# Rebuilt transform tables, a last unit gated by token groups and a new rule in the instruction planner of a fused adaLN, long-convolution and gMLP block

## The chip, the cores and the metric

One core of a Trainium2 chip runs the whole program. A core has five engines with queues of their own: TensorE (PE in the profile, with its weight loads as PEld), VectorE (DVE), ScalarE (ACT), GpSimd (POOL) and SyncE (SP, which here issues nearly all DMAs). Each engine takes its instructions strictly in order and waits on semaphores. The metric is the device time of one execution in microseconds; the median of several runs is compared.

## The reference

The input is x = A_q of 2048 tokens by 640 channels, in bfloat16. Six vectors of 640 come from one small product, `silu(c) @ w_mod`: shift, scale and gate for each of two halves.

```
h = layernorm(x) * (1 + ca) + sa
k_shift = 4-tap causal convolution of k along the tokens, per channel
kv = k_shift * v
y  = irfft(rfft(kv padded to 4096) * rfft(ssm_k padded to 4096))[:2048] + kv * ssm_D
x  = x + ga * h * y
h  = layernorm(x) * (1 + cb) + sb
z  = gelu(h @ w_in);  z1, z2 = halves of z (864 columns each);  z2 = layernorm(z2)
g  = w_sp @ z2 + b_sp            # over the tokens, 2048 x 2048
out = x + gb * ((z1 * g) @ w_out)
```

## The kernel before

**Stages.** The first part, some 224 us, computes everything up to z; the second part (lines 880 to 940) is a plain loop over 16 token tiles of the product with `w_sp` (`mix`, L905) and the product with `w_out` (`project`, L923). The second part isn't touched by the change.

**The long convolution** is done as matrix products. The 640 channels are 5 units of 128 (`NU`, `DU`). For each unit the filter (X named K) and the kv product (X named U) go through the same steps: `load_X` brings 512 KB in; `stage1` multiplies by a small table F1 (four pieces, each evacuated from PSUM to `X1`, L315); `forward` multiplies by slices of a 128 x 128 x 16 table of cosines and sines, `M2`. The filter's result is kept as `KH` (`k_item`). For the kv product, `u_item` multiplies its spectrum by KH on VectorE (`product`, L497, 40 of them), goes back with the transposed table `G2` (`inv`) and evacuates to `Z`. There are 8 such steps per unit. `last_stage` turns Z by a DMA transpose, and `y_mult` multiplies it by the table E and then, on VectorE, `gh` (the modulated first layernorm) by the result (L686). Only the last unit, u = 4, is turned on TensorE (`last_stage_pe`): four blocks of eight transposes, each with a copy to `ZTp` and its own `y_mult`. Each `y_mult` covers 32 channels of all 2048 tokens, so no token is complete before the fourth. Two of these four go through a ScalarE copy first (L681, L683).

**The tables.** `M2` is built in eight chunks (`m2_chunk`): three GpSimd instructions per chunk make the angle in turns and its rounding (L395, L397, L398), two on VectorE take the remainder and its absolute value (L402, L327), two Sin activations on ScalarE follow (L405, L407), and VectorE negates one of the parts (L409). `G2` is made from M2 by TensorE transposes (L422), a VectorE copy (L424) and a negation on GpSimd (L427). A block of G2 needs four chunks of M2, and `forward` step st needs chunk st. Silu, which the modulation vectors need, and a warming Gelu run on ScalarE ahead of these.

**The rest.** `load_kv` and `short_conv` make kv in a transposed layout (`taps` on TensorE with a diagonal `dg`, then `times_v` on VectorE, L561), write it to HBM, and read it as XU. `ln1` (statistics on VectorE, or on ScalarE at L580, L581), `xn`, `mod`, `gh_mod` (L658) and `resid` (L723) are the first layernorm, its modulation and the residual add. `resid` also takes the statistics of the second layernorm (L729), and for each of four token groups of 512 `z_group` finishes these (L795, and `rstd_from_var` on GpSimd, L234 and L235), normalises (L803), turns the tile (group 0 by TensorE with ScalarE modulating, L824 and L831; the others by a DMA transpose with VectorE, L816) and multiplies by `w_in`.

**The planner.** Nothing in the first part is in program order. Each piece of work is an `op` with one or more engines and a cost for each, its dependencies, the buffers it opens, and a wished time `t` from the table `WANT`. `Plan.run` walks forward in its own model of time: among all ops that are ready it picks the one that can start first, adding a handicap from `SECOND` where an op would go to an engine that isn't its first; `t` breaks ties. The order in which ops are picked is the order on the engines. Buffers of a kind come in a number of slots (`SLOTS`); those in `FIXED` are opened in the order in which the code names them. Where the model shows TensorE without work for long, `new` puts in filler products of `ident` with 512 columns (`plan.gap`), which compute nothing that is used and keep TensorE busy.

The key by which the planner chooses, and the line in which it does so:

```
key = (at + (o["alt"] if e != next(iter(o["eng"])) else 0), o["t"], i)
if best is None or key < best[0]:
```

## Time and profile before

| | us |
|---|---|
| median of 5 runs | 353.93 (353.86 to 354.36) |
| the profiled execution | 353.93 |
| its span, first to last instruction | 352.1 |
| TensorE busy, share of the span | 329.5, 94% |
| VectorE busy | 218.0, 62% |
| ScalarE busy | 147.4, 42% |
| GpSimd busy | 111.7, 32% |

The span runs from the first to the last instruction; the device time is 1.8 us longer. A busy TensorE is not a TensorE doing useful work: the fillers count as busy, and a matmul's recorded duration is longer than the time until the next can start. In the tables of instructions an L number is the line in the kernel that issued it; L293 is the helper through which most matmuls go, and L315 the helper for copies, so these are told apart by the names of the tiles (`sm<-ident` is a filler, `ZTp<-pu` the copy of a turned block). GpSimd's spans are rough.

### The profile page before, as it was taken

How to read it: one execution, taken by the hardware profiler on the slowest of the kernel's cores; microseconds unless marked ns; L12 is line 12 of the kernel's file. 1: busy time of each engine (PE TensorE's matmuls, PEld its weight loads, DVE VectorE, ACT ScalarE, POOL GpSimd, SP SyncE). 2: the span in 40 equal slices, each digit the busy share in tenths (PEclk: the TensorE clock that was granted, in tenths of full speed). 3: DMA queues.
4: the chain of work that ended last, by engine and by line, in shares of the span. 5: the costliest groups of instructions: out<-in, count | busy, mean ns of one | idle time of the engine just before them, and what ended most of it. 6: DMA issues, size and time to landing. Idle time of an engine off the chain costs nothing.

```text
span 352.1 us, 6835 instructions
## 1 busy us (share of the span) xinstructions
PE 329.5 (94%) x2819; PEld 211.3 (60%) x2826; DVE 218.0 (62%) x435; ACT 147.4 (42%) x243; POOL 111.7 (32%) x142
## 2 busy tenths in 40 slices
PE   7667999999996999897999999999999999999996
PEld 3235577877885899753555555555555555555554
DVE  7986598867589668999798678623223332232233
ACT  6467897886565675626555555200000000000000
POOL 7775130026899973661211014800000000000000
PEclk9999999999999899998999999999999999999999
DMA  7899993087829198530430896046764655531111
GB/s 123 183 280 253 204 348 83 2 212 197 198 80 231 59 236 166 154 93 2 75 63 13 129 181 190 0 97 144 96 152 104 106 125 121 119 98 47 45 47 56
DMA packets 128342, 45.02 MB, mean 128 GB/s; under 512 B 117592, under 2 KB 127672, under 8 KB 128312
## 3 DMA queue, kind: packets, MB, share of 16 engines
q1 hardware_dynamic: 127008, 44.59, 56.8%
q8 instruction: 22, 0.36, 0.4%
q10 hardware_dynamic: 1304, 0.00, 0.2%
q14 instruction: 8, 0.07, 0.0%
HBM read 16.11 MB, written 5.24 MB: 61 GB/s over the span
## 4 chain that ended last, share of the span: by engine, by line
PE 80%; DVE 8%; ACT 5%; POOL 3%; issue 2%; POOLq 0%; DVEq 0%; ACTq 0%
PE ps L905 27%; PE pz L293 18%; PE pu L293 18%; PE po L923 9%; PE sm L293 5%; PE s L293 4%; ACT X L315 2%; POOL T L398 1%; DVE st L729 1%; DVE T L497 1%; DVE xt L723 1%; DVE gh L686 1%; ACT KH L315 1%; POOL T L397 1%; ACT Z L831 1%
## 5 line engine op out<-in xcount | busy, mean ns | idle before, releaser
L905 PE MATMUL ps<-X,wT 128*128 128x432 bf16 x512 | 95.7, 346 | 0.0
L905 PEld LDWEIGHTS <-wT 128*128 128x128 bf16 x512 | 50.0, 98 | 42.3
L497 DVE TENSOR_TENSOR T<-pu,KH 128x1024 bf16<-128x1024 f32 x40 | 48.5, 1222 | 15.1 <-PE pu L293 10.4
L916 ACT COPY uT<-pt 128x896 bf16<-128x896 bf16 x1 | 0.9, 905 | 118.9 <-PE pt L915 118.9
L293 PEld LDWEIGHTS <-Z 128*128 128x128 bf16 x320 | 31.4, 98 | 27.6 <-issue 0.8
L293 PE MATMUL pu<-X,M 128*128 128x128 bf16 (+1 forms) x480 | 45.7, 239 | 0.2
L293 PE MATMUL pz<-T,G 128*128 128x128 bf16 (+1 forms) x480 | 42.6, 240 | 3.4 <-DVE T L497 3.3
L315 ACT CAST X<-s 128x1024 bf16<-128x1024 f32 x40 | 40.8, 1020 | 11.3 <-PE s L293 10.8
L293 PEld LDWEIGHTS <-G 128*128 128x128 bf16 x480 | 35.7, 99 | 7.3 <-issue 3.6
L293 PEld LDWEIGHTS <-M 128*128 128x128 bf16 x480 | 35.5, 98 | 5.8 <-issue 0.2
L908 DVE SCALAR_TENSOR_TENSOR u<-ps,bcol,G 128x432 bf16<-128x432 f32 x18 | 12.0, 668 | 42.2 <-PE ps L905 42.2
L293 PE MATMUL pu<-big,Z 128*128 128x432 bf16 x160 | 34.6, 348 | 0.0
L293 PE MATMUL pz<-big,Z 128*128 128x432 bf16 x160 | 34.4, 346 | 0.0
L923 PE MATMUL po<-w_o,uT 128*128 128x320 bf16 (+1 forms) x224 | 32.8, 299 | 0.0
L315 ACT CAST Z<-pz 128x512 bf16<-128x512 f32 x40 | 23.5, 590 | 17.2 <-PE pz L293 17.1
L908 DVE SCALAR_TENSOR_TENSOR u<-ps,bcol,M 128x432 bf16<-128x432 f32 x14 | 9.4, 668 | 31.5 <-PE ps L905 31.5
L923 PEld LDWEIGHTS <-uT 128*128 128x128 bf16 (+1 forms) x224 | 21.8, 98 | 9.8
L658 POOL TENSOR_TENSOR gh<-gh,gca_bf 128x512 bf16<-128x512 bf16 x20 | 23.2, 1170 | 9.0 <-DVE gca_bf L645 9.0
L862 DVE BATCH_NORM_STATS2 stz<-X 128x6 f32<-128x432 bf16 x32 | 18.8, 599 | 10.1 <-ACT X L856 9.5
L315 ACT CAST KH<-pu 128x512 bf16<-128x512 f32 x40 | 23.1, 605 | 3.9 <-PE pu L293 3.6
L925 DVE TENSOR_TENSOR ot<-po,xt 128x320 bf16<-128x320 f32 x32 | 15.7, 491 | 13.4 <-PE po L923 13.4
L658 POOL TENSOR_TENSOR gh<-gh,gsa_bf 128x512 bf16<-128x512 bf16 x20 | 23.0, 1160 | 2.7 <-DVE gsa_bf L648 1.6
(132 smaller groups left out, 380.4 us busy)
## 6 DMA issues: line engine op xcount, KB each, us to landing
wm<-in_w_mod_dram SPq DMA_DIRECT2D x6, 800.0 KB, 5.1
X<-in_A_ssm_k_dram SPq DMA_DIRECT2D x5, 512.0 KB, 6.0
kv_scr<-big SPq DMA_DIRECT2D x5, 512.0 KB, 5.5
xt<-in_A_q_dram SPq DMA_DIRECT2D x4, 640.0 KB, 5.7
X<-kv_scr SPq DMA_DIRECT2D x5, 512.0 KB, 4.7
out_dram<-ot SPq DMA_DIRECT2D x16, 160.0 KB, 2.5
big<-in_B_w_in_dram SPq DMA_DIRECT2D x2, 1080.0 KB, 6.3
w_o<-in_B_w_out_dram SPq DMA_DIRECT2D x6, 160.0 KB, 2.9
```

The source lines that it names most:

```text
L293: nc.tensor.matmul(o, lhsT=w, rhs=x, start=start, stop=stop)
L315: (e.copy if e is nc.scalar else e.tensor_copy)(dst, src)
L397: e.tensor_scalar(tl[v][:], tl[v][:], pidx[:, 0:1], 1.0 / 8192.0, op0=ALU.mult, op1=ALU.mult)
L398: e.tensor_scalar(tl[r][:], tl[v][:], MAGIC, MAGIC, op0=ALU.add, op1=ALU.subtract)
L497: e.tensor_tensor(T_[:], tl[pu][:, :, :, None, :].to_broadcast([P, KP, 2, 2, DU]), tl[KH][:, :, None, :, :].to_broadcast([P, KP, 2, 2, DU] ...
L658: lambda e, vec=vec, o=o: e.tensor_tensor(gvu, gvu, vec[:, None, d0:d0 + du].to_broadcast([P, TB, du]), op=o),
L686: op({"DVE": dve_cost(512)}, lambda e: e.tensor_tensor(ghv, ghv, src(), op=ALU.mult), r=[py], w=gk, t=t)
L862: op({"DVE": 620}, lambda e, i=i, n=n, fc=fc: e.bn_stats(out=stz[:, n, fc, :], in_=tl[z2][:, i, fc * FC:(fc + 1) * FC]), r=[(z2, (i, fc))] ...
L905: nc.tensor.matmul(ps[:, :FC], lhsT=wTs[t][:, s_, :], rhs=tl["z2_%d" % (s_ // TB)][:, s_ % TB, fc * FC:(fc + 1) * FC], start=(s_ == 0), st ...
L908: nc.vector.scalar_tensor_tensor(u[:, sl], ps[:, :FC], bcol[:, t:t + 1], z1[t][:, sl], op0=ALU.add, op1=ALU.mult)
L923: nc.tensor.matmul(ps[:, :HS], lhsT=uTs[t][:fsz[ft], ft, :], rhs=w_o[:fsz[ft], ft, h * HS:(h + 1) * HS], start=(ft == 0), stop=(ft == NFT ...
L925: nc.vector.tensor_tensor(ot[:, h * HS:(h + 1) * HS], ps[:, :HS], xt[:, t, h * HS:(h + 1) * HS], op=ALU.add)
```

## The change

**The planner.** `op` gets a mark `port` for VectorE instructions that use the SBUF port that VectorE shares with GpSimd. In the plan, a GpSimd op and a marked VectorE op no longer overlap: each starts at the earliest when the other's is over. The choice among ready ops is no longer strictly by the earliest start: all candidates within `LOOK` = 31 ns of the earliest are compared by their wished time. The wished times are new (`WANT`), several hundred single ops get a correction of their own (`SHIFT`), the handicaps are new (`SECOND`), and many costs are adjusted.

**The tables.** Of M2 the angle is now a common base (`m2_base`, one iota and one multiplication) plus a step per chunk. A chunk is two `tensor_scalar` on VectorE (or GpSimd), one `scalar_tensor_tensor` over 512 elements, two Sin activations that take the step as their bias, and the negation. The negation for G2 and the diagonal of the short convolution may go to VectorE or GpSimd, with VectorE first. Silu and the warming Gelu move behind the last Sin.

**The last unit.** All four blocks are turned and copied first, into the four `T` buffers. Then for each token group of 512 there are 32 matmuls of 16 columns (128 in all instead of 32 of 64 columns) and one VectorE multiplication, which completes that group for the unit.

**Small ones.** In `ln1` the repair of statistics taken on ScalarE is a VectorE op for a whole run of tiles, and `nmr1` is one VectorE instruction instead of two on GpSimd. `norm` of the second layernorm may go to ScalarE. `ZTp` now has one slot, which holds the base.

The diff, without the numbers of the three tables and without adjusted costs:

```diff
+LOOK = 31
-SLOTS = dict(X=4, ..., ZTp=2, ...)
+SLOTS = dict(X=4, ..., ZTp=1, ...)
-SECOND = {"gh": 13421, "h2": 7734, "ln": 256, "res": 1494, "x1": 12998, "xn": 2029, "z": 19661, "zt": 22790}
+SECOND = {"dg": 1178, "g2": 29243, "gh": 23515, "h2": 25688, "ln": 8821, "m1": 16354, "m2": 5123, "res": 1875, "x1": 27814, "xn": 542, "z": 24289, "zt": 20107, "zx": 18935}
...
-                    key = (at + (o["alt"] if e != next(iter(o["eng"])) else 0), o["t"], i)
-                    if best is None or key < best[0]:
-                        best = (key, i, e, cost, max(at, landed) if o["flip"] else at)
+                    if e == "POOL" or (e == "DVE" and o["port"]):
+                        at = max(at, port)
+                    seen = at + (o["alt"] if k else 0)
+                    found.append((o["t"], seen, i, k, e, cost, max(at, landed) if o["flip"] else at))
+            first = min((f[1] for f in found), default=0)
+            best = min((f for f in found if f[1] <= first + LOOK), default=None)
...
+            if e == "POOL" or (e == "DVE" and o["port"]):
+                port = at + cost
...
+        mstep, mturn = small("mstep", 2 * NCH), small("mturn", 2 * NCH)
+        nc.vector.tensor_scalar(mstep[:, 0:NCH], fidx[:, 0:NCH], pidx[:, 0:1], 4.0 * KCH / 8192.0, op0=ALU.mult, op1=ALU.mult)
+        nc.vector.tensor_scalar(mstep[:, NCH:], mstep[:, 0:NCH], 0.25, None, op0=ALU.add)
+        nc.vector.tensor_scalar(mturn[:], mstep[:], TWO_PI, None, op0=ALU.mult)
...
+                new(a, "T", [P, 2, KCH, P], F32)
+                for h in range(2):
+                    e.tensor_scalar(tl[a][:, h], tl["mbase"][:], mstep[:, h * NCH + i:h * NCH + i + 1], MAGIC, op0=ALU.add, op1=ALU.add)
+            op({"DVE": 540, "POOL": 1000}, turns, r=["mbase"], w=[a], new=[(a, "T")], t=t, alt="m2", port=True)
+            op({"DVE": 650}, lambda e: e.scalar_tensor_tensor(tl[a][:], tl[a][:], MAGIC, tl["mbase"][:, None].to_broadcast([P, 2, KCH, P]),
+                                                              op0=ALU.subtract, op1=ALU.subtract), r=["mbase"], w=[a], t=t, port=True)
+            for h, o in ((0, 2), (1, 0)):
+                op({"ACT": 430}, lambda e, h=h, o=o: e.activation(M2[:, o, ks], tl[a][:, h], ACT.Sin, scale=-TWO_PI,
+                                                                  bias=mturn[:, h * NCH + i:h * NCH + i + 1]),
...
-            op({"POOL": 1200}, lambda e: e.tensor_scalar(flatG[:, o:o + 8, :], flatG[:, 8 * b:8 * b + 8, :], -1.0, 1.0,
+            op({"DVE": 350, "POOL": 1050}, lambda e: e.tensor_scalar(flatG[:, o:o + 8, :], flatG[:, 8 * b:8 * b + 8, :], -1.0, 1.0,
...
-            op({"DVE": 650} if dt == 0 else {"POOL": 1100}, diag, ...)
+            op({"DVE": 650} if dt == 0 else {"DVE": 650, "POOL": 1050}, diag, ..., alt="dg", port=True)
...
-                op({"ACT": act_cost(1024), "DVE": 750}, keep, ...)
-                y_mult(u, qb, ZT, 0, ("y%d" % u, b), b % 2 == 0)
+                op({"ACT": act_cost(1024), "DVE": 750}, keep, ...)
+            for g in range(NT // TB):
...
+                    for q in range(NQ):
+                        mm(pv[:, :, q // (NQ // 2), q % (NQ // 2), :], tl[ZTs[q // QB]][:, q % QB, :], Ebd[:, g * TB:(g + 1) * TB, :],
+                           True, True)
+                op(pe(*[16] * NQ), mul, r=ZTs + ["E"], w=[py], ...)
+                op({"DVE": dve_cost(512)}, lambda e, ghv=ghv, py=py: e.tensor_tensor(ghv, ghv, tl[py][:], op=ALU.mult),
+                   r=[py], w=[("gh", (u, g))], ...)
...
-        op({"ACT": 1500}, lambda e: e.activation(sc[:], c_bf[:], ACT.Silu), w=["silu"], t=("", -60))
+        op({"ACT": 1500}, lambda e: e.activation(sc[:], c_bf[:], ACT.Silu), r=["M2", "e2c", "F1"], w=["silu"], t=("silu", 0))
...
+            op({"DVE": 150}, lambda e: e.scalar_tensor_tensor(nmr2[:, gs], mv2[:, gs, 0], -1.0, rstd2[:, gs], op0=ALU.mult, op1=ALU.mult),
+               w=[("nm2", g)], r=[("rs2", g)], t=("zp_%d" % g, 0.5))
```

## The prediction

> **What bounds the kernel now.** First the page's totals and its rows of busy tenths (40 slices of 8.8 us).
>
> ```profile
> PE 329.5 (94%) x2819; PEld 211.3 (60%) x2826; DVE 218.0 (62%) x435; ACT 147.4 (42%) x243; POOL 111.7 (32%) x142
> ...
> PE   7667999999996999897999999999999999999996
> ...
> PEclk9999999999999899998999999999999999999999
> ```
>
> TensorE is the bound, but not evenly: slices 1 to 4, 13 and 17 to 18 are thin. I cut the span there, with the busy time of each engine in each stretch (after start:end come its length, PE, PEld, DVE, ACT, POOL, the granted clock, the DMA share and GB/s).
>
> ```profile
> 0.00:42.00 42.00, 32.26 (x253) 16.71 (x256) 30.74 (x85) 27.96 (x46) 26.12 (x49) 1.00 0.99 211
> 42.00:106.80 64.80, 63.73 (x823) 50.67 (x827) 51.46 (x83) 50.16 (x83) 28.97 (x40) 1.00 0.64 161
> 106.80:118.00 11.20, 8.01 (x103) 6.47 (x99) 9.56 (x9) 5.67 (x8) 10.81 (x11) 0.85 0.84 205
> 118.00:144.50 26.50, 26.42 (x414) 23.90 (x409) 21.29 (x24) 17.31 (x28) 17.96 (x16) 1.00 0.72 157
> 144.50:163.90 19.40, 14.76 (x176) 9.74 (x177) 18.79 (x55) 9.44 (x15) 8.43 (x9) 0.95 0.26 82
> 163.90:223.70 59.80, 59.80 (x325) 31.75 (x324) 47.70 (x116) 35.46 (x65) 15.39 (x19) 0.99 0.49 96
> ```
>
> From 163.9 on TensorE is full, and the change has nothing to take there: 59.8 us for z, then 128.4 to the end. Ahead of it I count what TensorE loses: idle time, fillers, low clock. In 0 to 42 it idles 9.74; of 35 fillers, 19 run slow at the start (5.86 us by the timeline) and 16 take 0.22 each (22 of them took 4.91 later on): 9.74 + 5.86 + 3.6 = 19.2. In 42 to 106.8: 1.1 idle and 8 fillers, 2.9. In 106.8 to 118: 3.2 idle, one filler, and 15% of 8.0 us for the clock, 4.6. In 118 to 144.5: 0.1. In the tail: 4.6 idle, 25 fillers 5.6, clock 0.7, together 10.9. Lost in all 37.7 of 163.9 us; so 126 us of useful work are left, and only the start, the hole and the tail can shrink.
>
> What holds each? For the start, the chain of work that ended last:
>
> ```profile
> 14.34 1.25 POOL dg L546
> ...
> 16.00 0.48 POOL T L397
> ...
> 16.56 1.11 POOL T L398
> 17.67 0.31 POOL T L395
> ```
>
> It runs on GpSimd from 10.5 to 24.0, through L395, L397 and L398 of chunk after chunk. For the hole, the timeline:
>
> ```profile
> 107.06 5.13 DVE L723 TENSOR_TENSOR xt<-xt,gh 128x512 bf16<-128x512 bf16 x4
> ...
> 113.37 1.22 PE L293 MATMUL pz<-T,G 128*128 128x256 bf16 x12 [2.87 <-DVE T L497]
> ```
>
> Four residual adds on VectorE take 5.13 us while GpSimd works; the same form takes 0.36 to 0.44 where GpSimd rests. The product (L497) queued behind them comes late, and TensorE waits 2.87 us. For the tail, the chain again:
>
> ```profile
> 144.51 0.59 ACT Z L315
> ...
> 148.90 1.79 DVE gh L686 x3
> ...
> 154.44 1.29 DVE xt L723
> ...
> 159.11 1.53 DVE Z L803 x4
> ...
> 161.00 2.22 ACT Z L831 x3
> ```
>
> The last inverse product ends at 144.5 and z starts at 163.9; VectorE is busy 18.8 of these 19.4 us, much of it with tokens that group 0 doesn't need.
>
> **What the Trainium skill says.** "SBUF — State Buffer", section Who interferes with whom: a VectorE instruction in a two-port mode, or with two SBUF inputs against a GpSimd one that reads SBUF, blocks fully until the other is over. The trace agrees: 1.25 to 1.37 us for the adds under GpSimd, about one GpSimd instruction (1.16) later. Products from PSUM stay at 1.21 to 1.23 throughout. "TensorE: Matmul & The Clock Gate", What's actually happening, has half clock after some 3.4 us of idleness; the records show 0.85 behind the hole. "ScalarE: Activation LUTs", What ACT_TABLE_LOAD costs, gives 1283 ns for a load; this trace has five of 1.28.
>
> **The change part by part.** Against the profiled execution, 353.93 with its span of 352.1 (1.8 outside it); the median is the same number.
>
> *Tables.* GpSimd loses per chunk 0.355 + 0.496 + 1.101 = 1.95 us, 15.6 in all. VectorE had 0.427 + 0.578 + 0.321 = 1.33 (10.6 in all, with port waits). Now it has two fp32 `tensor_scalar` of 256, a form that no row shows on VectorE: by "VectorE: DVE Perf Modes", section Side-by-side, two elements a cycle and some 150 cycles fixed, 0.29 each (an estimate; 0.42 if it runs at one a cycle, as L327 does). The `scalar_tensor_tensor` over 512: L327's undisturbed 0.42 plus 256 elements at 0.96 GHz, 0.69. The negation undisturbed 0.22. Sum 1.49, 11.9 in all, bounded by 10.5 and 14. `m2` has VectorE first and a handicap of 5.1 us on GpSimd, so I put all of it on VectorE. There too go four G2 negations (1.04 on GpSimd; 0.42 from the 256-element form plus 768 at four per cycle) = 1.7, up to four diagonals at 0.77 = 3.1, and three small step instructions ahead of the plan, 0.6. The E table sheds port waits: its two one-element instructions of 0.87 and 0.51 against 0.16 for their like (L347), 1.1.
>
> VectorE's need from 4.9 us (F1 done) to the end of M2: a diagonal 0.8, E 2.7, M2 11.9, four `times_v` 2.7: 18.1, so 23.0 instead of 26.9, when the last negation ended. Half of it suffices for the first steps. ScalarE is free earlier: its first Sin waited at 8.8 behind three loads for Silu, Gelu and Sin again (3 x 1.28 and two activations of 0.2, from 4.5). The two that stay come behind the last Sin: 3.0 us on ScalarE just where it is busy (8.96 of 10 us in 30 to 40). `times_v` of the first kv tile, which began at 11.63 though its taps ran from 7.9, may begin 3 us earlier, and with it the write, the read of XU and the kv `stage1` (29.6 to 36.8 before). The new wishes also load the first filter block ahead of the second kv tile (-1045 against -53), past SP's four transposes. The first product L497 came at 41.5; VectorE (23), ScalarE (its work up to there is 22 + 3 us from 2.8) and the XU read allow 31 to 36. Not all is gain: some taps that filled TensorE before 20 us come later. I take **-5.5**, bounded by 0 (VectorE simply replaces GpSimd) and -9 (at 31 us about 20 of useful work fit, so 10 are lost instead of 19.2).
>
> *Hole.* With the port rule a GpSimd-first op never starts earlier on VectorE while GpSimd is working, and the handicap of 1.9 us decides for GpSimd. So the five residual adds of units 0 to 3 on VectorE move: +5 x 1.16 = 5.8 us for GpSimd, which has shed 15.6 + 4.1 + 4.4 and so has room; if it had none, residuals would come late, but only the tail waits for them. I take **-3.5** of the 4.6, bounds -4.6 and 0.
>
> *Tail.* From the last inverse product: Z copy 0.6, first flips 0.65, four copies on ScalarE (handicap 20 us on VectorE) 4 x 1.02, 32 matmuls of 16 columns. That size is in no row; eight of 64 columns take 0.23 to the next group, so 0.03 each gives 0.9; the TensorE page (Wait — 56ns, not 53.3ns?) has a floor of 25 ns whatever the size, 0.8, so both ends agree, and the 96 additional matmuls cost 2.8 us, under fillers. Then 0.68 (L686), 0.44 (add), four statistics and aggregates at 0.42 = 1.7, GpSimd 1.5, the new `nm2` 0.2, norm 1.5, flips 0.4, ScalarE modulating 3.7: 16.4 with 0.5 for hops, against 19.4: -3. But z of group 1 must follow: group 0 takes 16 x 0.913 = 14.6 us, to 178.5, and group 1's tile was ready at about 177.4 (its transpose issued at 169.54, 5.8 to landing, five times 0.41). That is 1.1 of slack, and VectorE is busy 24.4 of 25.5 us from 144.5 to 170; nine statistics of later groups (0.37 each) can stand back. I take **-2.5**, bounds -4 and 0.
>
> *Friction.* First-layernorm statistics leave ScalarE (handicap 8.8 instead of 0.26): four tiles at 1.15 = 4.6 us more for VectorE, with two diagonals in 40 to 66, where it was busy 22.6 of 26: 28.7 needed, 2.7 too many; from 33.3 to 42 it was idle 5.4. I take **+1.5**, bounds 0 and +8.
>
> Sum: -5.5 - 3.5 - 2.5 + 1.5 = -10.0. Span 342.1, time **343.9**. Removed table loads, shorter GpSimd rstd and the unused ScalarE norm I cost at nothing: they are covered by TensorE's 102 nearly full microseconds from 42 to 144.5, or are in the sums.
>
> **Rivals.**
> *VectorE replaces GpSimd in the start* (-1 instead of -5.5): for it, VectorE is busy 24.9 of 28.4 us from 4.9 to 33.3 already; against it, half of M2 suffices. 348.4.
> *The tail gives nothing*, since group 1 comes no earlier (slack 1.1): 346.4.
> *Everything works* at its far bound without friction, -9 - 4.6 - 4: 336.3.
> *Slower: VectorE becomes the bound from 5 to 66 us.* It was busy 49 of 61 there. M2 +1.3, G2 +1.7, diagonals +3.1, statistics +4.6, less E's 1.1: 58.6. Being in order, each product behind a batch of these is late, and TensorE waits. The start gains nothing, friction +8, hole -3.5, tail -2.5: +2, 355.9. It decides when friction passes 6 us with no gain in the start. Against it, products stand early in the wishes (t 0 to 40; statistics 3424).
>
> **How the numbers follow.** Forecast 0.43 (its own range 341 to 347), VectorE in the start 0.22, no tail 0.10, everything 0.13, slower 0.10, within 0.2% (353.2 to 354.6, about what this kernel's measurement can tell from no change) 0.02. Faster is 0.43 + 0.22 + 0.10 + 0.13 = 0.88. The range leaves out the slower case and half of the best one: 336.5 to 351.5.
>
> **What would show it.** M2 chunks without GpSimd and its last Sin before 23; first L497 by 36; no VectorE block of adds at over 1 us each; z starting near 154; three table loads. Wrong: TensorE waiting for L497 in 40 to 66, `tensor_scalar` of the chunks above 0.42, fillers as many as before, or TensorE idle between z groups 0 and 1.

## The result and the profile after

| | before | after |
|---|---|---|
| median, us | 354.97 (80 runs) | 354.21 (43 runs) |
| ratio of the two | | 0.9946 [0.9930, 0.9962] |
| profiled execution, us | 353.93 | 354.21 |
| its span, us | 352.1 | 352.2 |

By the ratio the change makes the kernel about 1.9 us faster, where 10 were predicted; the forecast of 343.9 and the upper end of its range, 351.5, both lie below what was measured. Executions of one kernel lie up to 5.7 us apart here (350.12 to 355.78 for the changed one), and the ratio is one of fast runs, which leaves out the ten slowest of the changed kernel and none of the kernel before; over all executions the means are 1.3 us apart and the medians 0.8. So the two profiled executions, which are equally long (that of the kernel before is 1.0 us under its median), are no contradiction to the ratio. They serve to say where time went, and the ratio says how much.

The page of the changed kernel, its totals, TensorE's row of busy tenths and the granted clock:

```profile
PE 332.6 (94%) x2923; PEld 213.7 (61%) x2929; DVE 219.9 (62%) x465; ACT 139.2 (40%) x225; POOL 89.9 (26%) x101
...
PE   7559899999999999997999999999999999999996
...
PEclk9978999999999999998999999999999999999999
```

The dent of the hole (a 6 in the thirteenth place before) is gone, that of the tail (an 8 and a 7) is down to one 7, and GpSimd has lost 21.8 us of work. The thin slices at the left edge are still there, 7559 where 7667 stood. The same stages as in the prediction, with the columns as there:

```profile
0.00:42.00 42.00, 31.54 (x224) 16.18 (x226) 33.46 (x108) 23.42 (x39) 2.56 (x15) 0.92 0.90 192
42.00:106.80 64.80, 63.67 (x784) 48.35 (x788) 52.76 (x86) 45.25 (x67) 38.37 (x37) 1.00 0.83 165
106.80:118.00 11.20, 11.20 (x167) 9.74 (x168) 8.66 (x10) 8.58 (x12) 4.14 (x5) 1.00 0.94 248
118.00:144.50 26.50, 25.75 (x392) 23.09 (x390) 24.12 (x37) 17.79 (x28) 20.51 (x19) 1.00 0.58 154
144.50:163.90 19.40, 16.04 (x307) 12.53 (x304) 15.77 (x44) 9.60 (x16) 5.71 (x6) 0.97 0.29 87
```

The hole is full (11.20 of 11.20 at full clock instead of 8.01 at 0.85). In the first 42 us TensorE issues 224 products instead of 253, fillers counted in, at a clock of 0.92. How far the work had come is told best by events that both kernels have: the products `T<-pu,KH` on VectorE (40), the last evacuation of `Z`, the first product of z with `w_in`, the first with `w_sp`.

| stretch | before, us | after, us | difference | predicted |
|---|---|---|---|---|
| start to the 1st product | 41.51 | 47.76 | +6.3 | -5.5 |
| 1st to 24th product | 64.41 | 64.91 | +0.5 | friction, +1.5 |
| 24th to 25th (the hole) | 6.19 | 1.18 | -5.0 | -3.5 |
| 25th to the end of the last Z | 32.98 | 33.85 | +0.9 | |
| last Z to the first product of z (the tail) | 19.83 | 16.45 | -3.4 | -2.5 |
| z to w_sp | 58.59 | 59.43 | +0.8 | |
| w_sp to the end | 128.64 | 128.62 | 0.0 | 0 |

The first row, on VectorE, before and after:

```profile
41.51 2.35 DVE L497 TENSOR_TENSOR T<-pu,KH 128x1024 bf16<-128x1024 f32 x2 [0.26 <-PE pu L293]
47.76 1.21 DVE L605 TENSOR_TENSOR T<-pu,KH 128x1024 bf16<-128x1024 f32 x1
```

Before rounding the rows sum to +0.05, the difference of the spans. Hole and tail gave about what was foreseen; the start lost instead of gaining, and ate both. The two orders differ between the 1st and the last product too, so the cut at the 24th and 25th is sharper than the work: from the 1st product to the last Z it is 3.6 us less in all. The 0.8 us in z go with the clock at z's first products: 0.77 granted from 163 to 170 us, 0.84 before; a run below that keeps this part of the order (the one without fillers in the chain) has 1.00 there and takes 58.52 from z to w_sp.

For the hole, GpSimd's timeline: the four residual adds of a unit now run there, where VectorE had taken such a block at 107.06, and no product stands behind them.

```profile
104.59 4.49 POOL L841 TENSOR_TENSOR xt<-xt,gh 128x512 bf16<-128x512 bf16 x4 [0.69 <-DVE gh L789]
```

For the tail, the chain of work. Two multiplications of the last unit (L830) stand in it ahead of group 0's residual add (L841), and it is 3.4 us shorter from the last Z on:

```profile
147.12 0.59 ACT Z L406
...
149.54 0.70 DVE gh L789
...
153.29 1.20 DVE gh L830 x2
154.49 0.02 issue
154.51 0.64 DVE xt L841
...
158.60 1.44 DVE Z L929 x4
...
160.46 2.12 ACT Z L957 x3
```

What is different in the start? ScalarE's timeline after:

```profile
28.79 1.01 ACT L406 CAST X<-s 128x1024 bf16<-128x1024 f32 x1 [1.69 <-PE s L384]
29.70 0.91 ACT L513 ACTIVATE M<-T,mturn 128x256 bf16<-128x256 f32 x2
30.91 0.58 ACT L406 CAST KH<-pu 128x512 bf16<-128x512 f32 x1 [0.30 <-PE pu L384]
...
38.09 1.28 ACT L870 ACT_TABLE_LOAD   x1
...
41.01 0.99 ACT L406 CAST X<-s 128x1024 bf16<-128x1024 f32 x1
```

and TensorE's:

```profile
20.38 1.02 PE L384 MATMUL s<-ident 128*128 128x512 bf16 x4 [1.29 <-ACT X L406]
21.33 0.40 PE L384 MATMUL s<-F1bd,X 64*128 64x128 bf16 x8
22.83 1.87 PE L384 MATMUL s<-ident 128*128 128x512 bf16 x4 [1.10 <-ACT X L406]
24.63 0.61 PE L384 MATMUL s<-F1bd,X 64*128 64x128 bf16 x8
26.34 1.86 PE L384 MATMUL s<-ident 128*128 128x512 bf16 x4 [1.10 <-ACT X L406]
28.14 0.61 PE L384 MATMUL s<-F1bd,X 64*128 64x128 bf16 x8
```

VectorE has its last M2 angle ready at 23.99, close to the 23.0 of the prediction. But the last two sines run at 29.70. ScalarE takes its queue in order, and ahead of them stands the fourth evacuation of the first filter's `X1`, which waits for TensorE, which first computes four fillers (`s<-ident`) ahead of each piece. The first `KH` is ready to be copied at 30.9, as before (31.0). From there to the first product it takes 16.9 us instead of 10.5: the fourth evacuation of the kv product stands behind two table loads, and 32 products of the short convolution of kv1 and kv2, which the kernel before did at 15.7 to 20.7 and 36.5 to 40.5, stand in TensorE's queue from 40.9 to 51, because SP loads kv1 at 22.6 instead of 6.9.

That gives four suspects for the start: the lean tables themselves (V: VectorE takes GpSimd's place), the fillers (F), the table loads (C), the late taps (A). For the tail there is the question what carries it: the gate, or the order.

### The profile page after: what moved, and what is told of

Its sections match the earlier page's. It is cut to its first block, busy times and chain, and to the rows that moved or that the text cites. A ratio compares the mean times of both kernels' runs of the same rounds, so it can differ in the third digit from the quotient of the medians.

```text
span 352.2 us, 6998 instructions
## 1 busy us (share of the span) xinstructions
PE 332.6 (94%) x2923; PEld 213.7 (61%) x2929; DVE 219.9 (62%) x465; ACT 139.2 (40%) x225; POOL 89.9 (26%) x101
## 4 chain that ended last, share of the span: by engine, by line
PE 83%; DVE 9%; ACT 5%; issue 2%; POOL 1%; ACTq 0%; DVEq 0%; POOLq 0%
PE ps L1031 27%; PE pz L384 18%; PE pu L384 17%; PE po L1049 9%; PE sm L384 7%; PE s L384 5%; ACT X L406 2%; DVE T L605 1%; ACT KH L406 1%; DVE st L692 1%; DVE st L847 1%; ACT Z L957 1%; DVE T L510 1%; DVE dg L654 1%; PE sm L530 1%
## 5 line engine op out<-in xcount | busy, mean ns | idle before, releaser
L605 DVE TENSOR_TENSOR T<-pu,KH 128x1024 bf16<-128x1024 f32 x40 | 47.8, 1218 | 8.1 <-PE pu L384 4.9
L406 ACT CAST X<-s 128x1024 bf16<-128x1024 f32 x40 | 40.9, 1022 | 13.0 <-PE s L384 12.9
L384 PE MATMUL pz<-T,G 128*128 128x128 bf16 (+1 forms) x480 | 41.5, 237 | 0.0
L384 PEld LDWEIGHTS <-G 128*128 128x128 bf16 x480 | 34.6, 98 | 3.1
L384 PE MATMUL pz<-big,Z 128*128 128x432 bf16 x160 | 32.8, 346 | 0.0
L1049 PEld LDWEIGHTS <-uT 128*128 128x128 bf16 (+1 forms) x224 | 21.8, 98 | 9.8
L1051 DVE TENSOR_TENSOR ot<-po,xt 128x320 bf16<-128x320 f32 x32 | 15.7, 492 | 13.4 <-PE po L1049 13.4
```

The source lines that it names most:

```text
L384: nc.tensor.matmul(o, lhsT=w, rhs=x, start=start, stop=stop)
L406: (e.copy if e is nc.scalar else e.tensor_copy)(dst, src)
L605: e.tensor_tensor(T_[:], tl[pu][:, :, :, None, :].to_broadcast([P, KP, 2, 2, DU]), tl[KH][:, :, None, :, :].to_broadcast([P, KP, 2, 2, DU] ...
L1049: nc.tensor.matmul(ps[:, :HS], lhsT=uTs[t][:fsz[ft], ft, :], rhs=w_o[:fsz[ft], ft, h * HS:(h + 1) * HS], start=(ft == 0), stop=(ft == NFT ...
L1051: nc.vector.tensor_tensor(ot[:, h * HS:(h + 1) * HS], ps[:, :HS], xt[:, t, h * HS:(h + 1) * HS], op=ALU.add)
```

## Experiments

In most of these kernels the planner runs first and its list (op, engine, number of fillers ahead) is then edited and issued, so that all that isn't named stays in its place. In the diffs `order` is this list. Executions with the same instructions in the start can differ there: three kernels below keep the start of the kernel before (the one with the adds on GpSimd, and the two with group 0 first), and have the first product at 41.50, 42.98 with the gate and 42.54 without, at a granted clock of 1.00, 0.83 and 0.83 from 10 to 20 us. So a single difference of up to 1.5 us in the start proves nothing; the ratios, each against the kernel before on the same chip, decide.

### Parts of the change in the kernel before

**The five residual adds.**

```diff
+for o in order:
+    if o.label in ("res0", "res1", "res2") and o.engine == "DVE":
+        o.engine = "POOL"
```

> The kernel before in its own order, with one edit: the five residual adds of units 0 to 2 that stood on VectorE (four of them the block of 5.13 us) are issued on GpSimd in the same place. If the hole at 107 to 118 us is due to the shared port, TensorE's wait of 2.9 us and the low clock behind it go: 3 to 4.5 us faster. Rival: GpSimd's later gh work makes the same product or the residuals late, and the time stays within 1 us.

0.9891 [0.9837, 0.9944], that is 3.9 us, and faster than the changed kernel. On VectorE the product behind the hole now waits for TensorE alone:

```profile
105.91 1.22 DVE L507 TENSOR_TENSOR T<-pu,KH 128x1024 bf16<-128x1024 f32 x1 [0.72 <-ACT Z L325]
109.64 2.35 DVE L507 TENSOR_TENSOR T<-pu,KH 128x1024 bf16<-128x1024 f32 x2 [2.50 <-PE pu L303]
```

The 25th product comes at 109.64 instead of 112.11. By the 40th product this execution is 4.0 us ahead, so the hole was about as priced (it is the fastest of only four, hence the wide interval), and five of some 440 VectorE instructions moved to GpSimd are worth about twice the whole change. The edit takes the adds off VectorE altogether. It doesn't separate the waiting for the shared port from the 1.5 to 1.8 us that four undisturbed adds would take there.

**The lean tables, planned anew by the old planner.**

```diff
-    v: iota, tensor_scalar, tensor_scalar (GpSimd); tensor_tensor, fold (VectorE)
+    base once; per chunk two tensor_scalar and one scalar_tensor_tensor (VectorE first)
+SECOND: "m1": 16354, "m2": 5123
```

> The kernel before with the lean M2 tables alone (planner rule, wishes and the place of Silu as before; the plan is made anew, so the order of the start changes). Theory A (the tables are good, and the changed kernel lost its start by the order in which kv tiles are loaded and multiplied): 2 to 6 us faster, first product L497 before 40 us. Theory B (VectorE, which now makes the tables, is the bound of the start): same or slower by up to 4 us, first product after 42 us.

1.0302 [1.0252, 1.0353]: the first product at 52.8, 11 us late, and never made up. It says little of the tables, since the old wishes with new costs give another order everywhere. Hence the next run.

**The lean tables in the place of the old ones**, order as before:

```diff
     # at the first GpSimd angle
+    iota; tensor_scalar           -> mbase
     # at each chunk's two VectorE instructions
-    tensor_tensor; fold
+    tensor_scalar; tensor_scalar; scalar_tensor_tensor
```

> The kernel before in its own order, with only the making of M2 changed in place: the base at the place of the first GpSimd angle, each chunk's two tensor_scalar and one scalar_tensor_tensor at the place of the two old VectorE instructions, the sines with the step as bias; nothing replanned, the five table loads kept. Theory S (as predicted: GpSimd's angles held the start, the lean ones free it by several us): last angle on VectorE at 21 instead of 25, first product at 37 to 39 instead of 41.5, 0.988 to 0.992 of before. Theory V (VectorE takes GpSimd's place; TensorE's order and XU's read hold the first product): first product at 40.5 to 42, 0.998 to 1.002. Slower would say that the lean chunks cost VectorE more than the waits they take away.

1.0036 [1.0019, 1.0053], 1.3 us slower, first product at 43.07. Theory S falls. Of V the mechanism is there, and the numbers lie a little above its ranges: VectorE is busy 19.2 of the 20 us from 10 to 30 (18.1 before), its last angle comes at 26.5, and the chain of work from 8 to 28 us runs mostly on VectorE, through the chunks and the multiplications by v, where it had run on GpSimd:

```profile
19.36 0.54 DVE T L416 x2
19.90 0.02 issue
19.92 0.69 DVE T L417
20.61 0.60 DVE big L576
21.21 0.54 DVE T L416 x2
```

Where the 1.3 us are lost this one execution can't say. Its clock from 10 to 20 us was 0.83, and at 0.83 the unchanged start has its first product at 42.54 and 42.98, only 0.1 to 0.5 us earlier. The 1.6 us at the first product are made good between the 25th and the 40th, where the clock from 114 to 118 is 1.00 instead of 0.57, and z takes 1.2 us longer at a clock of 0.65 (0.84 before). What is shown is that the lean tables in this place gain nothing.

**Both together:**

```diff
+lean tables in place
+res0, res1, res2 on GpSimd
```

> As the one before, with the five residual adds on GpSimd as well (alone 0.989). If the two gains are of different stages they add: theory S 0.977 to 0.981, theory V 0.987 to 0.991.

0.9928 [0.9904, 0.9952]. They add: 1.0036 and 0.9891 make 0.9927. So of these two parts one pays 3.9 us and the other costs 1.3.

### The tail

**The gate alone in the kernel before**, planned by the old planner:

```diff
-for b in 4 blocks of 32 channels: flips, copy, 8 products of 64 columns, multiply all tokens
+for b in 4 blocks: flips, copy
+for g in 4 token groups: 32 products of 16 columns, multiply this group
```

> The kernel before with one part of the change alone: the last unit turned first and multiplied by token groups; planner, wishes, tables and start as before. If the part is what I priced (tail lost 8.9 us of TensorE time before and 5.6 in the changed kernel), the time falls by 2 to 3.5 us, 0.990 to 0.994. If the tail of the changed kernel got shorter only by its new order, this part alone changes the time by less than 0.7 us.

1.0035 [1.0018, 1.0052], slower. In its chain VectorE computes all four multiplications, and statistics of other groups, ahead of group 0's last statistics: the old choice by earliest start doesn't ask which group is urgent. z starts at 166.96 instead of 164.92.

**The gate alone out of the changed kernel:**

```diff
-for g in 4 token groups: 32 products of 16 columns, multiply this group
+for b in 4 blocks: 8 products of 64 columns, multiply all tokens
+order: the second pair of multiplications right behind the first
```

> The changed kernel in its own order with the gate undone: the last unit's four VectorE multiplications cover 32 channels of all tokens again (32 matmuls of 64 columns), so all four stand ahead of group 0's residual add instead of two. Theory G (the gate carries the shorter tail): two multiplications of 0.6 us come ahead of group 0 and z starts 1.2 to 2 us later, 0.998 to 1.000 of before. Theory O (the new order and the quiet GpSimd carry it; the gate added before alone gave nothing): z starts no more than 0.6 us later, 0.993 to 0.996.

0.9992 [0.9975, 1.0009] against 0.9946: the gate is worth 1.6 us here by the ratios, and 1.1 by the start of z. Its chain, to be read beside the one of the changed kernel above:

```profile
153.29 2.39 DVE gh L846 x4
155.68 0.02 issue
155.71 0.44 DVE xt L858
```

Two multiplications (1.2 us) more stand ahead of the residual add, and z starts at 165.27 instead of 164.15. So the gate pays in the changed kernel's order and not in the old one. Of the tail's 3.4 us it carries 1.1; the rest lies in the other edits there, which were not taken apart.

**Group 0 first in the kernel before**, with and without the gate, and with the adds on GpSimd. What group 0's normalisation needs goes ahead of everything else from the last product on:

```diff
+first = all that the normalisation of group 0 needs
+order[last product : its normalisation] = [in first] + [the others]
```

> The kernel before with its own order, but: the five residual adds on GpSimd (alone 0.989), the last unit gated by token groups (alone 1.0035), and from the last product to the normalisation of group 0 all that group 0's normalisation needs stands first on each engine. Theory T1 (the gate is worth its 2.5 us once VectorE's order serves group 0 first, which the old planner did not do): z starts 2.5 to 3.5 us earlier than with the adds alone, 0.980 to 0.983. Theory T2 (the work displaced comes back between the groups of z, since VectorE is full to 170): z starts earlier but TensorE idles between its groups, 0.987 to 0.991.

> As the one before, but with the last unit as in the kernel before (four blocks of 32 channels, no gate): the adds on GpSimd and the order alone. Theory T1: group 0 still needs all four blocks, so the order alone gives at most 1 us over the adds alone, 0.986 to 0.989, and the gate makes the rest. Theory T3 (order is all): as good as with the gate, within 0.3 us.

With the gate 1.0086 [1.0056, 1.0116], without it 1.0013 [0.9993, 1.0032], where the adds alone gave 0.9891. All theories fall: with group 0 first in this way, the gate made the kernel slower by some 2.6 us. Group 0's reciprocal roots are ready at 156.04 in the run with the gate; then the others, pushed back in a block, meet the normalisation. Its timeline, VectorE and GpSimd:

```profile
156.01 7.03 POOL L764 TENSOR_TENSOR xt<-xt,gh 128x512 bf16<-128x512 bf16 x6
156.07 4.85 DVE L844 TENSOR_SCALAR Z<-xt,mv,rstd 128x640 bf16<-128x640 bf16 x4 [1.44 <-POOL rstd L261]
```

Four instructions take 4.85 us, 1.21 each, beside GpSimd adds of 1.17; in the changed kernel, with GpSimd at rest, the same four take 1.51. This is the exclusive lock that the Trainium skill describes ("SBUF — State Buffer", Who interferes with whom), met by a `tensor_scalar` of one input, and it is a case that the new rule keeps apart in the plan: this normalisation is marked `port`. Then z's flips waited 3.8 us more for multiplications of other groups, which use the same `sm` buffers.

### The start

**Silu's table load early** (suspect C), in the changed kernel:

```diff
+order: Silu behind the cosine of the E table (8 us instead of 38)
-order: the warming Gelu
```

> The changed kernel with one thing moved: Silu, with its table load, runs right behind the cosine of the E table (about 8 us, where ScalarE waits for the first angles anyway) instead of at 38.1, and the warming Gelu is left out, so that Gelu's table is loaded at its first use in z. Theory C (the two loads and their activations, 38.09 to 41.1, hold the fourth evacuation of X1 of the kv product, and with it the first products): that evacuation at 38.8 instead of 41.0, first product at 45.5 instead of 47.8, 2.0 to 2.5 us less, about 0.989 of before. Theory A (the taps of kv1 and kv2, which stand in TensorE's queue at 41 to 51, hold the products whatever ScalarE does): first product unchanged within 0.5 us, about 0.994 of before. If the first use of Gelu in z waits for its load on the path that sets the end, up to 1.3 us are lost again: z's first groups would show an idle TensorE.

0.9973 [0.9950, 0.9995], no better than the changed kernel. The fourth evacuation did come at 38.7 instead of 41.0, as C said, and the first product at 47.64: the loads were covered by the taps that TensorE had to do anyway. C falls.

**The second kv tile early** (A):

```diff
+order: load of kv1 behind XK0; its taps and multiplications between the first filter's pieces
+order: kvw1 behind them; no fillers ahead of these taps and of pieces 2 to 4
```

> The changed kernel in its own order with one group of edits: the second kv tile is loaded right behind the first filter block on SP, and its four tap products, their multiplications by v and the write to HBM move from 41 to 52 us to 19 to 30 us, in place of the fillers there. Theory A (useful TensorE work was pushed out of the thin start): 3 to 5 us faster than the changed kernel. Theory B (VectorE bound): the four multiplications of 0.68 us delay the tables, no gain or up to 2 us slower. Theory C (the two table loads of ScalarE at 38 to 41 us hold the start): within 1 us.

0.9982 [0.9965, 0.9999], first product at 49.2. TensorE has no fillers left from 20 to 30 us, and it helps nothing: the multiplications by v now stand among the last chunks of M2 on VectorE, the taps wait for them and the pieces for the taps; the fourth is evacuated at 28.3 instead of 28.8. A falls as a cause of its own.

**Both:**

```diff
+Silu early, kv1 early
```

> Both moves in the changed kernel: Silu early as above, and the load of the second kv tile right behind XK0, with its taps at 19 to 28 us. The early taps alone gave nothing (0.998 of before). Theory C+A (taps were a loss too, but stood behind the table loads): more than Silu alone, 3.5 to 4.5 us less than the changed kernel, about 0.982 to 0.985 of before, first product at 44. Theory C alone (taps only take the place of fillers): no better than Silu alone, 0.989 to 0.994. If moving the taps delays the last angles on VectorE, as the first product of the early taps alone (49.2) suggests, it is worse than Silu alone.

0.9913 [0.9880, 0.9947], about 1.2 us less than the changed kernel, with overlapping intervals; in the profile the first product is at 47.44 and no later event more than 0.5 us earlier than in the changed kernel. Not told apart from nothing.

**No fillers in the chain** (F):

```diff
+for o in order:
+    if o.label in ("k0", "u0") and o.engine == "PE":
+        o.fillers = 0
```

> The changed kernel with the same order, but without the fillers that the planner put ahead of the stage1 pieces of the first filter and kv blocks. There is one s1 buffer, and a filler opens it for the piece behind it, so it starts only when ScalarE has evacuated the piece before: in the chain each of the second, third and fourth pieces carries 4 fillers (1.0, 1.9 and 1.9 us). Theory F (these fillers hold the first filter, and behind it in ScalarE's queue the last sines): last evacuation of the first filter at 24 to 25 instead of 28.8, last Sin at 26 to 27 instead of 29.7, first KH at 27 instead of 30.9, first product at 44 instead of 47.8, 3 to 4 us less than the changed kernel, about 0.985 of before. Theory V (VectorE and the taps hold the start in any case): first KH no more than 1 us earlier or the gain lost before the first product, 0.993 to 0.996.

0.9882 [0.9852, 0.9911], 2.3 us less than the changed kernel. F holds, with a smaller gain than foreseen. TensorE's timeline:

```profile
21.04 0.61 PE L400 MATMUL s<-F1bd,X 64*128 64x128 bf16 x8 [1.10 <-ACT X L422]
22.75 0.61 PE L400 MATMUL s<-F1bd,X 64*128 64x128 bf16 x8 [1.10 <-ACT X L422]
24.73 0.61 PE L400 MATMUL s<-F1bd,X 64*128 64x128 bf16 x8 [1.37 <-ACT X L422]
```

The pieces follow each other by 1.7 to 2.0 us instead of 2.6 to 3.5, first `KH` at 28.5, first product at 45.24. The filler opens the one `s1` buffer for the piece behind it, so it can't run in the gap that it is meant to fill: it waits for the same evacuation and then delays the piece by its own time. The price is the clock, 0.53 from 20 to 30 us, but with the fillers it was no more than 0.66 there. The Trainium skill, "TensorE: Matmul & The Clock Gate", section What's actually happening, has half speed after an idle window of some 3.4 us; the half speed is in this trace, but TensorE's gaps ahead of these pieces are 1.1 to 2.1 us, so this run doesn't show what sets it. The run with the early taps, 1.0% slower, kept 12 of the 24 fillers on `s`, so it differs from this one by these too.

**More fillers out, and Silu early:**

```diff
+for o in order:
+    if o.label in ("k0", "u0", "fk0", "g2", "taps1", "taps2") and o.engine == "PE":
+        o.fillers = 0
+Silu early
```

> As the one before, with the fillers ahead of the first forward steps, the G2 flips and the taps of kv1 and kv2 left out too (10 of them at 38.7 to 41.0), and Silu at 8 us. Theory F: the gains add up, first product at 42 to 43, 0.980 to 0.984 of before, unless TensorE's clock falls in the gaps where the fillers were (a granted clock under 0.9 in 42 to 52 would show that). Theory V: 0.991 to 0.995, as with the early Silu and the taps.

0.9903 [0.9870, 0.9936], the same within the intervals, first product at 46.40, with the clock at 0.68 from 10 to 20 and 0.50 from 20 to 30. The gains don't add up.

**VectorE's queue ahead of M2.**

```diff
+as without fillers ahead of k0, u0
+order: the E table and the second diagonal behind the last chunk of M2 (VectorE)
+18 fillers ahead of the first taps instead of 22
```

> The changed kernel without the fillers ahead of the stage1 pieces of the first filter and kv blocks (alone 0.988), and on VectorE the E table and the second diagonal, 5.4 to 8.2 and 9.0 to 9.6 us, moved behind the last chunk of M2; the fillers ahead of the first taps are 18 instead of 22. Theory V (what is left of the loss in the start is VectorE's queue, from F1 to the last chunk without a pause): base of M2 at 6.5 instead of 9.6, last angles at 20.5 instead of 23.3, first KH at 26 instead of 28.5, first product at 42.5 to 43.5 instead of 45.2, 0.980 to 0.984 of before. Theory W (the read of XU, issued behind the write of kv, and the taps of kv1 and kv2 hold the first product whatever VectorE does): first product at 45 or later, 0.987 to 0.990.

0.9829 [0.9783, 0.9876], 349.34 us in four executions: by its ratio the fastest of all, ahead of the kernel before by 6.1 us and of the changed one by some 4.2. The base of M2 begins at 6.3 instead of 9.6 and the last angles at 20.7, as V said; the first `KH` at 27.3 and the first product at 44.36, between the two theories. A new wait stands in ScalarE's queue (and so in front of the last four sines), the E table's cosine:

```profile
22.83 0.31 ACT L448 ACTIVATE e2c<-fr,halfpi 128x16 f32<-128x16 f32 x1 [2.08 <-DVE fr L442]
23.05 0.89 ACT L537 ACTIVATE M<-T,mturn 128x256 bf16<-128x256 f32 x2
```

**And that out of the way too:**

```diff
+order: the E table behind the last Sin; Silu behind the F1 cosine, no warming Gelu
+no fillers ahead of kv1's taps
```

> The last run before, with three further moves: the E table behind the last Sin and the first filter's last evacuation in the order of all engines (in that run its cosine stood at 22.83 in ScalarE's queue ahead of the last five sines, and ScalarE waited 2.1 us for it), Silu with its load right behind the F1 cosine at 5 us and no warming Gelu, and no fillers ahead of the taps of kv1. Theory V (VectorE's queue was the holder, and the next ones are ScalarE's, the E cosine and then the two loads at 35.3 to 38.2): last Sin at 22 instead of 25.2, first KH at 25.5 instead of 27.3, fourth evacuation of X1 of the kv product at 33 to 34 instead of 38.2, first product at 41 to 42 instead of 44.4, 0.974 to 0.979 of before. Theory W (the taps of kv1 and kv2 in TensorE's queue hold the products, and the loads are covered by them, as the early Silu alone showed): 0.981 to 0.985.

0.9868 [0.9840, 0.9895]. All early steps came as V said (first `KH` at 26.6, the fourth kv evacuation at 33.6 instead of 38.2), and the first product at 45.23, later than in the run before. TensorE:

```profile
35.35 0.40 PE L413 MATMUL s<-F1bd,X 64*128 64x128 bf16 x8
38.95 1.02 PE L413 MATMUL sm<-big,dg 128*128 128x512 bf16 x4 [3.19 <-DVE big L698]
```

It waits 3.2 us for a multiplication by v, behind six tiles' statistics that fill VectorE from 32.3 to 38.2.

**The statistics behind the second kv tile:**

```diff
+order: first-layernorm statistics, all but two instructions, behind kv1's multiplications
```

> The last run before with one move: the statistics of the first layernorm, which stood on VectorE at 29.2 to 38.2, all but the first two instructions, go behind the multiplications by v of the second kv tile. In that run its first taps were done at 34.5 and TensorE idled 3.2 us for the multiplication at 38.25. Theory V (VectorE's queue is the holder at each place in turn): the wait goes, first product at 41.5 to 42.5 instead of 45.2, 0.974 to 0.980 of before; if the statistics then make the modulation late, less. Theory W (the taps and XU hold the products): first product at 44 or later, 0.984 to 0.988.

0.9992 [0.9980, 1.0005]. The wait moves to the third kv tile and doubles:

```profile
47.92 1.86 PE L424 MATMUL sm<-big,dg 128*128 128x512 bf16 x4 [6.98 <-DVE big L709]
```

**Four tiles' statistics on ScalarE**, as in the kernel before:

```diff
+order: statistics of tiles 0 to 3 on ScalarE, one behind each evacuation of the second filter
```

> The run with the late E table and the early Silu (0.9868, first product 45.2), with one move: the statistics of tokens tiles 0 to 3, four of the nine that VectorE had ahead of the second kv tile at 38.25, go to ScalarE (two activations each, some 1.9 us a tile by the kernel before), one behind each of the four evacuations of the second filter. This is the term friction of the prediction taken alone: the kernel before had four tiles' statistics on ScalarE. Theory V (VectorE's amount of work, not only its order, holds the start): the multiplications of the second kv tile come 4 us earlier, TensorE's wait of 3.2 us goes without a new one behind it, first product at 42 to 43, 0.975 to 0.981 of before. Theory W (the taps and XU): first product at 44.5 or later, 0.984 to 0.988.

0.9957 [0.9943, 0.9970]. The first product comes at 40.40, earlier than in any kernel above, and the second at 49.65, because the repair of these statistics and the roots stand between them on VectorE:

```profile
46.11 0.17 DVE L750 TENSOR_SCALAR mv<-sums 128x8 f32<-128x8 f32 x1 [3.30 <-ACT gh L737]
...
48.73 0.99 DVE L760 SCALAR_TENSOR_TENSOR nmr<-mv,rstd 128x8 f32<-128x8 f32 x1 [2.06 <-POOL rstd L373]
49.65 1.21 DVE L653 TENSOR_TENSOR T<-pu,KH 128x1024 bf16<-128x1024 f32 x1
```

**The repair behind the sixth product:**

```diff
+order: repair, roots and the first eight normalisations behind the sixth product
```

> The last run with one move: the repair of the statistics taken on ScalarE, the reciprocal roots on GpSimd and the first eight normalisations, which stood on VectorE ahead of the second product and waited there for ScalarE (3.3 us) and GpSimd (2.1 us), go behind the sixth product of the first unit. In the last run the first product came at 40.4 instead of 45.2, and the second only at 49.6. Theory V (VectorE's work in the start, and nothing behind it, is what the change lost there): the second product at 42 to 43 and no TensorE wait over 1 us for VectorE to 60, 0.974 to 0.979 of before. If the modulation on GpSimd, which follows the normalisations, is then late for the first multiplications by E, the gain comes back as waits after 60: 0.981 to 0.986.

0.9904 [0.9874, 0.9934]. The second product is at 42.7 and the sixth at 52.1, and then the same sequence stalls there: VectorE waits 2.1 us for the roots at 55.85, ScalarE 2.75 for what follows, TensorE 2.6 for ScalarE. The 24th product, at 112.39, is back where the changed kernel has it (112.67). The gain came back as waits between 52 and 70.

## Why the prediction was wrong

*Hole.* Right: -3.5 foreseen. From the first product to the last Z the adds alone gave -4.0, and the changed kernel -3.6 with all else that it moves there (the cut at the 24th and 25th product alone shows -5.0). The adds of units 0 to 3 are all on GpSimd (1.15 each), those of unit 4 on VectorE take 0.46 each, and the edit alone gave 3.9 us.

*Tail.* Right in size, -3.4 against -2.5, and partly by luck. The parts listed for it come to 16.35 without the 0.5 for hops, so the -3 should have been -2.5. The half us taken off on top was for group 1 and VectorE's full queue; z did lose 0.8, but with the clock. Not as argued, either: the sum took the gate to shorten VectorE's path by itself, with one multiplication ahead of group 0's add. Two stand there, the gate alone made the kernel slower, and it pays only together with the new order. z starts at 164.2, not near 154, because the 40th product is 2.4 us late instead of some 7 early.

*Friction.* Foreseen +1.5 for VectorE's additional work. Behind the first product little of it shows: some 0.3 us to the last Z, if the adds give the 4.0 that they gave alone. Ahead of the first product, where I had not looked for it, the run with four tiles' statistics on ScalarE has it 4.8 us earlier, but that gain was lost again at the second product. So how much the statistics cost is not shown.

*Start.* This is the step that failed: "The first product L497 came at 41.5; VectorE (23), ScalarE (its work up to there is 22 + 3 us from 2.8) and the XU read allow 31 to 36." The sum for VectorE was right. M2 took 11.9 us there as worked out (5.5 + 4.9 + 1.5), the last angle came at 23.99, `tensor_scalar` at 0.346, inside its bounds:

```profile
L510 DVE SCALAR_TENSOR_TENSOR T<-T,ZTp 128x512 f32<-128x512 f32 x8 | 5.5, 691 | 0.2
L508 DVE TENSOR_SCALAR T<-ZTp,mstep 128x256 f32<-128x256 f32 x16 | 4.9, 346 | 0.0
...
L517 DVE TENSOR_SCALAR M<-M 128x256 bf16<-128x256 bf16 x8 | 1.5, 219 | 0.0
```

What was wrong is the step from "the angles are ready" to "the first product is": -5.5 us foreseen for it, +6.3 measured. I took each engine's amount of work as the bound and 31 to 36 from it as the time. Between lie queues in order, and the runs show three things in them:

1. Fillers ahead of the pieces of the first filter and kv blocks, in the same buffer as the piece: 2.5 us of the first product, 2.3 us of the time. They pushed the last sines behind them to 29.70.
2. The E table and a diagonal ahead of M2 on VectorE: another 0.9 us of the first product and of the profiled execution; by the ratios about 1.9 us of the time, with overlapping intervals.
3. VectorE's amount of work up to the first products. In place of the old ones, with nothing else changed, the lean tables gained nothing and the kernel was 1.3 us slower. Four orders (the last four runs) in which something was pulled ahead of something else on VectorE, or off it, gave TensorE a new wait each time, of 2.6 to 7.0 us, for what had been pushed back or for what follows it.

The first two make up 3.4 of the 6.3 us. The third is the likeliest holder of the rest. With four tiles' statistics taken off VectorE the first product did come at 40.40, which speaks for it; but the time behind it was lost again, so for the whole it is argued, not shown.

That third point is what two of the rivals said. "VectorE replaces GpSimd in the start" fits the tables in place, which gained nothing (+1.3, where it had -1). The slower rival, that VectorE becomes the bound from 5 to 66 us, comes close in the amount of work: it foresaw 58.6 us of work on VectorE; measured are 52.9 in the changed kernel, with 8 products and 12 multiplications by v where the kernel before had done 10 and 15. The two and three that are missing would take 2.4 and 2.0 us, so 57.3 for the same work, of 61.1; before it was 49.2. Statistics grew as said:

```profile
L692 DVE BATCH_NORM_STATS2 st<-xt 128x6 f32<-128x320 bf16 x26 | 11.1, 470 | 0.0
L605 DVE TENSOR_TENSOR T<-pu,KH 128x1024 bf16<-128x1024 f32 x8 | 9.7, 1218 | 1.0 <-PE pu L384 1.0
L669 DVE TENSOR_TENSOR big<-sm,big 128x512 bf16<-128x512 f32 x12 | 7.9, 678 | 1.0 <-PE sm L384 1.0
```

(26 instructions instead of 18, 11.1 us instead of 7.7). I gave this rival 0.10 because the wishes put products ahead of statistics. They do; but the multiplications by v, on which the taps' buffers and so TensorE wait, stand behind statistics: at 42.21 in the changed kernel, right behind eight tiles' statistics since 33.07, where taps that are late themselves still hide it, and at 38.25 in the run with the late E table and the early Silu, where TensorE waits 3.2 us.

Of the signs named, these showed the failure: more fillers than before (60 against 39 in the first 60 us), the last Sin at 30.6 and the first L497 at 47.8. TensorE waited less than 1 us for the products in 40 to 66; it was busy with taps that were late. Three table loads, M2 without GpSimd, no block of adds over 1 us each, and no gap between z's groups 0 and 1 came as predicted.

What stays open: no order of the changed kernel that was tried brings the 24th product ahead of 109.3, where the kernel before has it at 105.9. Other orders were not tried, so it is not shown that the lean tables can't be placed better. How the new rule of the planner by itself, without the new wishes, would do was not tried.

## What to carry to other kernels

Moving work from a busy engine to one that "has room" is paid in the order of its queue, so follow what stands behind the moved work to the instruction that sets the end, instead of comparing sums per engine. A filler must not need the buffer, or wait for the event, of the work it stands ahead of. And try the parts of a change alone: here five moved adds gave about twice what the whole gave.

## What the hardware showed unexpectedly

The same instructions at the start ran with a granted clock of 1.00 or 0.83 from 10 to 20 us in different executions, and the first product came 1.0 to 1.5 us later in those with 0.83 (41.50, 42.54, 42.98). A VectorE normalisation of 128 x 640 in bfloat16 takes 0.38 us with GpSimd at rest and 1.21 beside its adds, so a block of four costs 3.3 us more. Taking 23 fillers out of the start's chain lowered the clock from 20 to 30 us only from 0.66 to 0.53 and was a gain all the same.
